# A decode kernel's tail: last weight load in six transfers, output rows in four column groups gathered in PSUM, one copy and two stores at the end

## The chip, the cores and the metric

The kernel runs on one core of one Trainium2 chip. The metric is the device time of one execution in microseconds; lower is better. The span of a profile is about 2 us shorter than the time of the same run, because the time also holds what lies outside the profiled span. In the profile's lines PE is TensorE, PEld its weight loads, DVE VectorE, ACT ScalarE, POOL GpSimd and SP SyncE; a q behind a name is that engine's instruction queue, which issues transfers. SBUF is the on-chip memory of 128 partitions, PSUM the one that PE writes its products to. The granted clock is the share of PE's full clock that the chip allowed in a stretch.

## The reference, cut to what matters

```python
x = A_x                                             # (2, 1, 1024), batch of two, one token
g = sigmoid((x * gate_w).sum(-1, keepdims=True))
a = attention(x, k_cache, v_cache, wq) @ wo         # 32 heads, 16384 cached keys of 128, for each of two batches
b = mixer_mlp(B: x, w1..w4)                         # ends as x1 + h2
return g * a + (1 - g) * b                          # (2, 1, 1024)
```

The two caches are 537 MB together in bf16; with the weights the kernel reads 570 MB, each byte once. The last thing that happens is `o @ wo`: a (2 x 4096) by (4096 x 1024) product whose 8 MB of weights are the last bytes to be loaded.

## The kernel before

All large loads go through a ring of four 4 MB slots in SBUF, issued from one queue (SyncE) in a fixed order: weights of the projections, then keys and values of 64 (head, batch) pairs, last `wo` in two loads of 4 MB. The second of these is cut in three transfers of 3, 0.5 and 0.5 MB, each with a semaphore of its own, so that the products can start before all is there:

```python
wloads[("wo", pi)] = [wo_load(k0, kn - 1), wo_load(k0 + kn - 1, 1, 0, 2), wo_load(k0 + kn - 1, 1, 2, 2)]
wo_chunks.append(((("wo", pi), 0), [(c, r) for c in range(k0, k0 + kn - 1) for r in range(R4)]))
for t in range(2):
    wo_chunks.append(((("wo", pi), 1 + t), [(k0 + kn - 1, 2 * t + r) for r in range(2)]))
```

The output rows of the two batches are cut in halves of 512 columns. Half `hf` stands on PSUM partitions `32*hf` and `32*hf+1`, so the two matmuls of a weight row use two column groups of the PE array. (`c, r` name a row block of 128 weight rows: 4 `c` times 4 `r` in one load of 4 MB.)

```python
for c, r in crs:
    for hf in range(2):
        ev = pl.add("pe", lambda e, ...: e.matmul(
            rows_ps[32 * hf:32 * hf + 2, 0:HD2], lhsT=OT4_sb[:, r, c, :], rhs=wt[:, c % CPS, r, hf * HD2:(hf + 1) * HD2],
            start=first, stop=True, tile_position=(0, 32 * hf), ...), waits=w, sig=True)
```

The gate and the other half of the sum come in with the last VectorE instruction; then two stores, one from SyncE's queue and one from ScalarE's, each of two partitions:

```python
for hf, eng in enumerate(("sp", "act")):
    sl = slice(32 * hf, 32 * hf + 2)
    if hf == 0:
        ev_fin = pl.add("dve", lambda e: e.scalar_tensor_tensor(orow[:, :], rows_ps[0:PR, 0:HD2], grow[0:PR, 0:1], bgrow[:, :],
                                                                op0=ALU.mult, op1=ALU.add), waits=(ev_alast, evd["bg"]), sig=True)
    ev_out = pl.dma(eng, lambda e, sl=sl, hf=hf: e.dma_start(out[:, 0, hf * HD2:(hf + 1) * HD2], orow[sl, :]), s_out[hf],
                    waits=(ev_fin,))
```

## Time and profile before

| what | value |
|---|---|
| time, median of the first three runs | 1333.75 us (1333.74 to 1333.94) |
| profiled span | 1332.0 us |
| DMA engines busy | 99.7% of 16 engines' span |
| last byte of the last load | 1328.23 us |
| from there to the start of the last VectorE instruction | 1.24 us |
| that instruction | 0.74 us |
| from its end to the end of the span | 1.75 us |

From the page of the kernel before: the busy tenths and GB/s of the DMA engines in 40 slices of the span, the packets of the load queue and of the instruction queue (count, MB, share), and one group of VectorE instructions (count, busy time, mean ns).

```profile
span 1332.0 us, 13845 instructions
...
DMA  9999999999999999999999999999999999999998
GB/s 403 428 428 432 431 432 434 428 434 429 434 432 432 433 429 433 430 434 432 432 433 428 433 431 433 433 429 435 428 434 431 431 435 429 432 430 435 431 429 337
...
q1 hardware_dynamic: 21428, 570.44, 99.7%
q8 instruction: 10, 0.16, 0.0%
...
L726 DVE TENSOR_SCALAR OTp<-ps,recip 128x1 bf16<-128x1 f32 x64 | 14.1, 221 | 162.8 <-PE ps L710 162.8
...
```

The DMA engines are full from the second slice to the second last, and the bytes are fixed. So what the other engines compute in the middle should not show in the time (the length of their programs can: e7 and e8 below). The last slice moves 337 GB/s, so the tail is where something can be had. The end of the chain of waits of the kernel before (start us, duration us, what):

```profile
...
1300.87 24.87 DMA ring<-in_A_wo_dram
...
1325.79 3.66 PE ps L747 x32
...
1329.47 0.74 DVE orow L780
```

And the same stretch in the timeline (start us, duration us, engine, line, operation, tiles, count; in brackets the idle time before it and what ended it):

```profile
...
1325.79 3.62 PE L747 MATMUL ps<-ring,OT_sb 128*2 128x512 bf16 x32 [2.56 <-DMA ring<-in_A_wo_dram]
1329.47 0.74 DVE L780 SCALAR_TENSOR_TENSOR orow<-ps,grow,bgrow 34x512 bf16<-34x512 f32 x1 [15.25 <-PE ps L747]
1330.24 0.33 SPq L782 DMA_DIRECT2D out_dram<-orow  x1
1330.25 0.26 ACTq L782 DMA_DIRECT2D out_dram<-orow  x1
```

PE starts when the 3 MB part is complete and works 3.66 us through the 32 matmuls of the load. The chain names only this first part. The trace's records of each DMA engine's completion tell the rest: the 0.5 MB parts are complete at 1326.99 and 1328.23, while PE still works on the first part. So PE ends at 1329.45, 1.22 us after the last byte.

### The profile page before, as it was taken

Reading aid. Unit: us, or ns where it says so; the run is one execution under the profiler, and the core shown is the slowest. Engines: PE = TensorE matmul, PEld = TensorE weight load, DVE = VectorE, ACT = ScalarE, POOL = GpSimd, SP = SyncE. Lnnn points to the kernel's source line nnn. Section 1 sums busy time; section 2 is a strip of 40 time slices with the busy share of each in tenths; the row PEclk is TensorE's granted clock in tenths of the full one; section 3 lists DMA queues with packets and bytes.
Section 4 is the critical chain, followed back from the end, with each engine's and each line's share of the span. In section 5 each row is a group of like instructions: output and inputs, shape, how many; then the busy total and the mean of one; then the engine's idle time right before and its main releaser. Section 6 shows DMA issues by size and latency. Waiting matters only on the chain.

```text
span 1332.0 us, 13845 instructions
## 1 busy us (share of the span) xinstructions
PE 853.7 (64%) x5330; PEld 332.3 (25%) x5330; DVE 758.9 (57%) x998; ACT 89.7 (7%) x195; POOL 33.0 (2%) x161
## 2 busy tenths in 40 slices
PE   3656666667666666766666666666666666666765
PEld 3322222222222222222222222222222222222222
DVE  1076566556656656665665566566556656655661
ACT  0000000000000000000000000000000000000000
POOL 2000000000000000000000000000000000000000
PEclk9989887788787879787887887887899697878877
DMA  9999999999999999999999999999999999999998
GB/s 403 428 428 432 431 432 434 428 434 429 434 432 432 433 429 433 430 434 432 432 433 428 433 431 433 433 429 435 428 434 431 431 435 429 432 430 435 431 429 337
DMA packets 21459, 570.64 MB, mean 428 GB/s; under 512 B 2235, under 2 KB 2243, under 8 KB 2502
## 3 DMA queue, kind: packets, MB, share of 16 engines
q1 hardware_dynamic: 21428, 570.44, 99.7%
q8 instruction: 10, 0.16, 0.0%
q14 instruction: 3, 0.02, 0.0%
q10 hardware_dynamic: 18, 0.01, 0.0%
HBM read 570.44 MB, written 0.00 MB: 428 GB/s over the span
## 4 chain that ended last, share of the span: by engine, by line
DMA 65%; PE 22%; DVE 11%; issue 2%; DVEq 0%; ACT 0%; POOL 0%; SPq 0%
DMA ring<-in_A_k_cache_dram 62%; PE ps L643 20%; DVE ring L631 10%; DMA ring<-in_A_wo_dram 2%; DMA ring<-in_A_wq_dram 2%; DVE OTp L726 1%; PE ps L460 0%; PE ps L747 0%; PE ps L589 0%; PE ps L489 0%; PE ps L710 0%; PE ps L381 0%; DVEq L71 0%; ACT P_sb L696 0%; DVE orow L780 0%
## 5 line engine op out<-in xcount | busy, mean ns | idle before, releaser
L643 PE MATMUL ps<-ring,Z 128*128 128x512 bf16 x2048 | 642.0, 467 | 338.9 <-DVE ring L631 328.3
L631 DVE STREAM_TRANSPOSE ring<-ring 128x1024 f32<-128x1024 f32 x512 | 590.9, 1211 | 129.2 <-DMA ring<-in_A_k_cache_dram 129.2
L643 PEld LDWEIGHTS ps<-ring,Z 128*128 128x128 bf16 x2048 | 206.8, 112 | 701.6 <-issue 358.8
L659 PE MATMUL ps<-ring,PT_sb 128*32 128x512 bf16 x2048 | 123.9, 384 | 3.1 <-DMA ring<-in_A_v_cache_dram 3.1
L696 ACT ACTIVATE P_sb<-ps,negm 128x512 bf16<-128x512 f32 x64 | 44.0, 687 | 1118.0 <-DVE negm L690 1118.0
L726 DVE TENSOR_SCALAR OTp<-ps,recip 128x1 bf16<-128x1 f32 x64 | 14.1, 221 | 162.8 <-PE ps L710 162.8
L668 DVE TENSOR_REDUCE rA<-ps 128x1 f32<-128x512 f32 x64 | 44.2, 691 | 90.0 <-PE ps L643 90.0
L702 DVE STREAM_TRANSPOSE PT_sb<-P_sb 128x512 bf16<-128x512 bf16 x64 | 45.5, 711 | 54.1 <-ACT P_sb L696 54.1
L659 PEld LDWEIGHTS ps<-ring,PT_sb 128*32 128x32 bf16 x2048 | 49.1, 97 | 46.8 <-issue 4.6
L675 PE MATMUL ps<-ident,rmax_bf 128*1 128x128 bf16 x64 | 13.9, 217 | 66.3 <-DVE rmax_bf L670 66.3
L705 ACT ACTIVATE acc_sb<-ps 128x512 bf16<-128x512 f32 x64 | 38.2, 597 | 55.1 <-PE ps L659 55.1
L728 POOL COPY OT_sb<-OTp 128x1 bf16<-128x1 bf16 x64 | 11.9, 186 | 1204.7 <-DVE OTp L726 1204.7
L675 PEld LDWEIGHTS ps<-ident,rmax_bf 128*1 128x1 bf16 x64 | 5.1, 79 | 97.9 <-DVE rmax_bf L670 97.9
L680 DVE TENSOR_REDUCE m_sb<-ps 1x1 bf16<-1x128 bf16 x64 | 18.0, 281 | 19.8 <-PE ps L675 19.8
L710 PEld LDWEIGHTS ps<-dsel,acc_sb 128*128 128x128 bf16 x256 | 20.4, 118 | 33.9 <-issue 30.0
L690 DVE TENSOR_SCALAR negm<-ps,cAB 128x1 f32<-128x1 f32 x64 | 17.7, 277 | 17.3 <-PE ps L685 17.3
L685 PE MATMUL ps<-m_sb,ones_bf 1*128 1x1 bf16 x64 | 11.0, 172 | 24.1 <-DVE m_sb L680 24.1
L717 PEld LDWEIGHTS ps<-rowsum,ones_f 128*128 128x128 f32 x128 | 19.0, 188 | 28.0 <-issue 26.8
L717 PE MATMUL ps<-rowsum,ones_f 128*128 128x1 f32 x128 | 24.5, 260 | 1.2 <-ACT P_sb L696 1.2
L722 DVE RECIPROCAL recip<-ps 128x1 f32<-128x1 f32 x64 | 10.7, 167 | 20.0 <-PE ps L717 20.0
L589 PE MATMUL ps<-xT_bf,ring 128*128 128x2 bf16 x256 | 7.1, 165 | 17.9 <-DMA ring<-in_A_wq_dram 17.9
L710 PE MATMUL ps<-dsel,acc_sb 128*128 128x1 bf16 x256 | 17.5, 172 | 1.1 <-ACT acc_sb L705 1.1
(91 smaller groups left out, 128.5 us busy)
## 6 DMA issues: line engine op xcount, KB each, us to landing
ring<-in_A_k_cache_dram SPq DMA_DIRECT2D x64, 4096.0 KB, 25.7
ring<-in_A_v_cache_dram SPq DMA_DIRECT2D x64, 4096.0 KB, 31.7
ring<-in_A_wq_dram SPq DMA_DIRECT2D x2, 4096.0 KB, 17.6
ring<-in_B_w_dram SPq DMA_DIRECT2D x2, 3584.0 KB, 32.4
ring<-in_B_w_dram SPq DMA_DIRECT2D x1, 4096.0 KB, 28.3
ring<-in_A_wo_dram SPq DMA_DIRECT2D x1, 4096.0 KB, 33.7
ring<-in_B_w_dram SPq DMA_DIRECT2D x1, 3072.0 KB, 27.4
ring<-in_A_wo_dram SPq DMA_DIRECT2D x1, 3072.0 KB, 24.9
```

What stands on the lines that cost most here:

```text
L631: ev_T[(g, u)] = pl.add("dve", lambda e: e.transpose(ap, ap), waits=(arrived(("k", g)),), sig=True)
L643: ev = pl.add("pe", lambda e, bp=bp: e.matmul(S_ps(pg)[:, 0:NCOL], lhsT=Z[:, pg, bp, ZO - 2 * u:ZO - 2 * u + P], rhs=kv[:, :, bp // 2, :, ...
L659: ev = pl.add("pe", lambda e, jj=jj, hf=hf, cg=cg: e.matmul(acc_ps[32 * cg:32 * cg + 32, 0:512], lhsT=PT_sb[:, pg, 32 * jj:32 * jj + 32], ...
L668: e1 = pl.add("dve", lambda e: e.tensor_reduce(rA[:, pg:pg + 1], S_ps(pg)[:, 0:NCOL], axis=AX.X, op=ALU.max), waits=(ev_S[g],), sig=True)
L675: ev_mt[g] = pl.add("pe", lambda e: e.transpose(mt_ps, rmax_bf[:, pg:pg + 1], ident[:, :]), waits=(ev_rmax[g], ev_m.get(g - 1), ev_ident i ...
L680: ev_m[g] = pl.add("dve", lambda e: e.tensor_reduce(m_sb[0:1, pg:pg + 1], mt_ps, axis=AX.X, op=ALU.max), waits=(ev_mt[g], ev_mb.get(g - 2) ...
L696: ev_P[g] = pl.add("act", lambda e: e.activation(P_sb[:, pg, :], S_ps(pg)[:, 0:NCOL], ACT.Exp, bias=negm[:, pg:pg + 1], scale=scale, accum ...
L702: ev_PT[g] = pl.add("dve", lambda e: e.transpose(PT_sb[:, pg, :], P_sb[:, pg, :]), waits=(ev_P[g], ev_PV.get(g - 2)), sig=True)
L705: ev_accc[g] = pl.add("act", lambda e: e.activation(acc_sb[:, :], acc_ps[:, 0:512], ACT.Copy), waits=(ev_PV[g], ev_ext.get(g - 1)), sig=True)
L710: ev = pl.add("pe", lambda e, w=w: e.matmul(oT_ps, lhsT=acc_sb[:, w * P:(w + 1) * P], rhs=dsel[:, w:w + 1], start=(w == 0), stop=(w == 3)) ...
L717: ev_l[g] = pl.add("pe", lambda e: e.matmul(l_ps, lhsT=ones_f[:, :], rhs=rowsum[:, pg:pg + 1], start=True, stop=True), waits=(ev_P[g], ev_ ...
L726: ev_OT[g] = pl.add("dve", lambda e: e.tensor_scalar(OTp[:, pg:pg + 1], oT_ps, recip[:, pg:pg + 1], None, op0=ALU.mult), waits=(ev_ext[g], ...
```

## The change

The intent: let PE follow the arriving bytes more closely (six transfers, the last one a quarter of a megabyte), do the row products in four column groups of 256 in place of two of 512, and make the last VectorE instruction shorter. For the last, the gate is folded into the normalisation of the heads, the other half of the sum, already gated, is written into the PSUM bank before the output products add to it, and only a copy of 256 columns remains. The diff, cut to its core:

```diff
-                wloads[("wo", pi)] = [wo_load(k0, kn - 1), wo_load(k0 + kn - 1, 1, 0, 2), wo_load(k0 + kn - 1, 1, 2, 2)]
-                ...
+                parts = [(c, 0, R4) for c in range(k0, k0 + kn - 1)] + [(k0 + kn - 1, 0, 2)]
+                parts += [(k0 + kn - 1, r, 1) for r in range(2, R4)]
+                wloads[("wo", pi)] = [wo_load(c, 1, r0, rn) for c, r0, rn in parts]
 ...
-            evd["bg"] = ... e.tensor_scalar(bgrow[:, :], bgrow[:, :], grow[0:PR, 1:2], None, op0=ALU.mult)
+            evd["bg"] = ... e.tensor_scalar(rows_ps[:, 0:DQ], bgrow[:, :], grow[:, 0:1], None, op0=ALU.mult)
 ...
-            ... e.tensor_scalar(OTp[:, pg:pg + 1], oT_ps, recip[:, pg:pg + 1], None, op0=ALU.mult)
+            ... e.tensor_scalar(OTp[:, pg:pg + 1], oT_ps, recip[:, pg:pg + 1], gT[:, pg:pg + 1], op0=ALU.mult, op1=ALU.mult)
 ...
-                    for hf in range(2):
-                            rows_ps[32 * hf:32 * hf + 2, 0:HD2], ..., rhs=wt[:, c % CPS, r, hf * HD2:(hf + 1) * HD2], start=first, ...
+                    for qd in range(NQ):                                # NQ = 4, DQ = 256
+                            rows_ps[32 * qd:32 * qd + 2, 0:DQ], ..., rhs=wt[:, c % CPS, r, qd * DQ:(qd + 1) * DQ], start=False, ...
 ...
-                ev_fin = ... e.scalar_tensor_tensor(orow[:, :], rows_ps[0:PR, 0:HD2], grow[0:PR, 0:1], bgrow[:, :], ...)
-            ev_out = ... e.dma_start(out[:, 0, hf * HD2:(hf + 1) * HD2], orow[sl, :])
+        ev_fin = pl.add("dve", lambda e: e.tensor_copy(orow[0:PR, :], rows_ps[0:PR, 0:DQ]), waits=(ev_alast,), sig=True)
+            ev_out = ... e.dma_start(out[b, 0, :].rearrange("(q n) -> q n", q=NQ), orow[b:PR:32, :])
```

The row products of the prologue (second mixer) go to four groups of 256 as well, and the input row comes in four small loads in place of two.

More of the change, by code (lines that the diff above doesn't have):

```diff
@@ L150, in build_kernel @@
     CPS = SLOT // (R4 * D)
-    HD2 = D // 2
-    PR = 34
-    assert H % HPC == 0 and HD2 <= 512
+    NQ = 4
+    DQ = D // NQ
+    PR = 32 * (NQ - 1) + 2
+    assert H % HPC == 0 and DQ <= 512
     with ExitStack() as st:
@@ L188, in build_kernel @@
         OT4_sb = sb("OT4_sb", [P, R4, NCT, 2], BF16)
-        xrow = sb("xrow", [PR, HD2], BF16)
-        bgrow = sb("bgrow", [PR, HD2], F32)
-        orow = sb("orow", [PR, HD2], BF16)
-        m22 = sb("m22", [P, 2, 2], F32)
+        xrow = sb("xrow", [P, DQ], BF16)
+        bgrow = sb("bgrow", [P, DQ], F32)
+        orow = sb("orow", [P, DQ], BF16)
+        m24 = sb("m24", [P, 2, NQ], F32)
         m2 = sb("m2", [P, 2], F32)
-        gm = sb("gm", [P, 2, 2], F32)
-        grow = sb("grow", [P, 2], F32)
+        gm = sb("gm", [P, 2], F32)
+        grow = sb("grow", [P, 1], F32)
         zz = sb("zz", [P, 2, NBD, 2], F32)
@@ L217, in build_kernel @@
         s_xr = sem("dxr")
-        s_tail = [sem(f"dtl{i}") for i in range(3)]
+        s_tail = [sem(f"dtl{i}") for i in range(CPS + 2)]
         pl = _Plan(esems)
@@ L251, in build_kernel @@
         pconst(lambda e: e.memset(Z[:, :, :, :], 0.0))
-        e0 = pconst(lambda e: e.memset(m22[:, :, :], 0.0))
-        pconst(aff(m22[:, :, :], 0, [[-1, 2], [-32, 2]], 1), (e0,))
+        e0 = pconst(lambda e: e.memset(m24[:, :, :], 0.0))
+        pconst(aff(m24[:, :, :], 0, [[-1, 2], [-32, NQ]], 1), (e0,))
         ev_xr0 = pconst(lambda e: e.memset(xrow[:, :], 0.0))
@@ L257, in build_kernel @@
                     waits=(ev_rowm,), sig=True)
-        pl.add("dve", lambda e: e.tensor_reduce(m2[:, :], m22[:, :, :], axis=AX.X, op=ALU.add), waits=(ev_const,))
+        pl.add("dve", lambda e: e.tensor_reduce(m2[:, :], m24[:, :, :], axis=AX.X, op=ALU.add), waits=(ev_const,))
         pl.add("dve", lambda e: e.tensor_scalar(cAB[:, 0:1], rowv[:, :], -scale, None, op0=ALU.mult), waits=(e0,))
@@ L329, in build_kernel @@
             else:
-                wloads[("wo", pi)] = [wo_load(k0, kn - 1), wo_load(k0 + kn - 1, 1, 0, 2), wo_load(k0 + kn - 1, 1, 2, 2)]
-                wo_chunks.append(((("wo", pi), 0), [(c, r) for c in range(k0, k0 + kn - 1) for r in range(R4)]))
-                for t in range(2):
-                    wo_chunks.append(((("wo", pi), 1 + t), [(k0 + kn - 1, 2 * t + r) for r in range(2)]))
+                parts = [(c, 0, R4) for c in range(k0, k0 + kn - 1)] + [(k0 + kn - 1, 0, 2)]
+                parts += [(k0 + kn - 1, r, 1) for r in range(2, R4)]
+                wloads[("wo", pi)] = [wo_load(c, 1, r0, rn) for c, r0, rn in parts]
+                for t, (c, r0, rn) in enumerate(parts):
+                    wo_chunks.append(((("wo", pi), t), [(c, r0 + r) for r in range(rn)]))
         def q_load(key):
@@ L395, in st_gate @@
                               waits=(e4,), sig=True)
-            e5 = pl.add("dve", lambda e: e.tensor_tensor(gm[:, :, :], gT[:, :].rearrange("p (t b) -> p t b", b=2),
-                                                         m2[:, :].unsqueeze(1).broadcast_to([P, 2, 2]), op=ALU.mult),
+            e5 = pl.add("dve", lambda e: e.tensor_tensor(gm[:, :], gT[:, 2:4], m2[:, :], op=ALU.mult),
                         waits=(evd["g"], ev_const), sig=True)
-            evd["grow"] = pl.add("dve", lambda e: e.tensor_reduce(grow[:, :], gm[:, :, :], axis=AX.X, op=ALU.add), waits=(e5,), sig=True)
+            evd["grow"] = pl.add("dve", lambda e: e.tensor_reduce(grow[:, :], gm[:, :], axis=AX.X, op=ALU.add), waits=(e5,), sig=True)
         def ln_a(z_ap, zkey, st_ps, tag):
@@ L487, in run @@
                 for kl in kls:
-                    for hf in range(2):
-                        ev = pl.add("pe", lambda e, kl=kl, hf=hf, st=row_first[0]: e.matmul(
-                            rows_ps[32 * hf:32 * hf + 2, 0:HD2], lhsT=lhs_of(k0 + kl), rhs=wv[:, kl, hf * HD2:(hf + 1) * HD2],
-                            start=st, stop=True, tile_position=(0, 32 * hf), skip_group_check=True),
-                            waits=w, sig=(kl == kls[-1] and hf == 1))
+                    for qd in range(NQ):
+                        ev = pl.add("pe", lambda e, kl=kl, qd=qd, st=row_first[0]: e.matmul(
+                            rows_ps[32 * qd:32 * qd + 2, 0:DQ], lhsT=lhs_of(k0 + kl), rhs=wv[:, kl, qd * DQ:(qd + 1) * DQ],
+                            start=st, stop=True, tile_position=(0, 32 * qd), skip_group_check=True),
+                            waits=w, sig=(kl == kls[-1] and qd == NQ - 1))
                         w = ()
@@ L501, in st_bg @@
             evs = []
-            for hf in range(2):
-                sl = slice(32 * hf, 32 * hf + 2)
-                c1 = pl.add("dve", lambda e, sl=sl: e.tensor_tensor(bgrow[sl, :], rows_ps[sl, 0:HD2], xrow[sl, :], op=ALU.add),
-                            waits=(evd["rows"], ev_xr, ev_bg0), sig=True)
-                evs.append(c1)
-            evd["bg"] = pl.add("dve", lambda e: e.tensor_scalar(bgrow[:, :], bgrow[:, :], grow[0:PR, 1:2], None, op0=ALU.mult),
+            for qd in range(NQ):
+                sl = slice(32 * qd, 32 * qd + 2)
+                evs.append(pl.add("dve", lambda e, sl=sl: e.tensor_tensor(bgrow[sl, :], rows_ps[sl, 0:DQ], xrow[sl, :], op=ALU.add),
+                                  waits=(evd["rows"], ev_xr, ev_bg0), sig=True))
+            evd["bg"] = pl.add("dve", lambda e: e.tensor_scalar(rows_ps[:, 0:DQ], bgrow[:, :], grow[:, 0:1], None, op0=ALU.mult),
                                waits=tuple(evs) + (evd["grow"],), sig=True)
@@ L543, in build_kernel @@
         ev_gw = pl.dma("act", lambda e: e.dma_start(gw_row[0:1, :], gate_w.rearrange("(o d) -> o d", o=1)), s_gw)
-        for hf in range(2):
-            ev_xr = pl.dma("act", lambda e, hf=hf: e.dma_start(xrow[32 * hf:32 * hf + 2, :], A_x[:, 0, hf * HD2:(hf + 1) * HD2]), s_xr,
+        for qd in range(NQ):
+            ev_xr = pl.dma("act", lambda e, qd=qd: e.dma_start(xrow[32 * qd:32 * qd + 2, :], A_x[:, 0, qd * DQ:(qd + 1) * DQ]), s_xr,
                            waits=(ev_xr0,))
@@ L725, in do_OT @@
             pg = g % 2
-            ev_OT[g] = pl.add("dve", lambda e: e.tensor_scalar(OTp[:, pg:pg + 1], oT_ps, recip[:, pg:pg + 1], None, op0=ALU.mult),
+            ev_OT[g] = pl.add("dve", lambda e: e.tensor_scalar(OTp[:, pg:pg + 1], oT_ps, recip[:, pg:pg + 1], gT[:, pg:pg + 1], op0=ALU.mult,
+                                                               op1=ALU.mult),
                               waits=(ev_ext[g], ev_rc[g], ev_OTc.get(g - 2)), sig=True)
@@ L740, in do_aproj @@
             ev_o4 = pl.add("dve", lambda e: e.tensor_copy(OT4_sb[:, :, :, :], o4_ps), waits=(ev,), sig=True)
-            first = True
             for (key, k), crs in wo_chunks:
@@ L745, in do_aproj @@
                 for c, r in crs:
-                    for hf in range(2):
-                        ev = pl.add("pe", lambda e, c=c, r=r, hf=hf, wt=wt, first=first: e.matmul(
-                            rows_ps[32 * hf:32 * hf + 2, 0:HD2], lhsT=OT4_sb[:, r, c, :], rhs=wt[:, c % CPS, r, hf * HD2:(hf + 1) * HD2],
-                            start=first, stop=True, tile_position=(0, 32 * hf), skip_group_check=True), waits=w, sig=True)
+                    for qd in range(NQ):
+                        ev = pl.add("pe", lambda e, c=c, r=r, qd=qd, wt=wt: e.matmul(
+                            rows_ps[32 * qd:32 * qd + 2, 0:DQ], lhsT=OT4_sb[:, r, c, :], rhs=wt[:, c % CPS, r, qd * DQ:(qd + 1) * DQ],
+                            start=False, stop=True, tile_position=(0, 32 * qd), skip_group_check=True), waits=w,
+                            sig=(qd == NQ - 1))
                         w = ()
-                    first = False
             return ev
@@ L776, in build_kernel @@
         ev_alast = do_aproj()
-        for hf, eng in enumerate(("sp", "act")):
-            sl = slice(32 * hf, 32 * hf + 2)
-            if hf == 0:
-                ev_fin = pl.add("dve", lambda e: e.scalar_tensor_tensor(orow[:, :], rows_ps[0:PR, 0:HD2], grow[0:PR, 0:1], bgrow[:, :],
-                                                                        op0=ALU.mult, op1=ALU.add), waits=(ev_alast, evd["bg"]), sig=True)
-            ev_out = pl.dma(eng, lambda e, sl=sl, hf=hf: e.dma_start(out[:, 0, hf * HD2:(hf + 1) * HD2], orow[sl, :]), s_out[hf],
+        ev_fin = pl.add("dve", lambda e: e.tensor_copy(orow[0:PR, :], rows_ps[0:PR, 0:DQ]), waits=(ev_alast,), sig=True)
+        for b, eng in enumerate(("sp", "act")):
+            ev_out = pl.dma(eng, lambda e, b=b: e.dma_start(out[b, 0, :].rearrange("(q n) -> q n", q=NQ), orow[b:PR:32, :]), s_out[b],
                             waits=(ev_fin,))
```

## The prediction

> **What bounds the kernel now.** The DMA engines. The page gives queue 1 99.7% of 16 engines' span; the 40 slices move 428 to 435 GB/s, only the first (403) and last (337) less. PE is 64% busy, VectorE 57%. Loads land 25 to 32 us after issue while one 4 MB load moves in under 10, so more than one is always queued. The 570 MB do not change. Only the tail after the last bytes is to be had.
>
> **The tail before** (chain of waits, timeline, the trace's records of each DMA engine's completion). The 3 MB part of the last load is complete at 1325.74, the two 512 KB parts at 1326.99 and 1328.23. PE starts its 32 matmuls of that load at 1325.79 and ends at 1329.45 (0.114 us each), because 24 of them wait for the 3 MB: 1.22 us after the last byte. The fused multiply-add takes 0.74 us, to 1330.21; stores and their completion 1.75 us, to 1331.96. Sum after the last byte: 3.73 us.
>
> **What the change does.**
> - Transfers of 1, 1, 1, 0.5, 0.25, 0.25 MB: PE works through each while the next lands; after the last one only 4 matmuls (256 columns, four column groups) remain. The Trainium skill (TensorEngine Tiling, Tiling Modes) lists four independent 128x32 tiles; this trace agrees: the PV product with four groups takes 1.94 us for 32 matmuls of 512 columns, the output rows with two groups 3.66. Estimate for 4 of 256: 0.3 us (one of 512 is shown as 0.38). PE ends 0.35 us after the last byte in place of 1.22. Gain 0.87.
> - One copy of 98x256 from PSUM in place of the 34x512 multiply-add (743 ns). A cast of 64 columns from PSUM took 225 ns, a reduction over 512 took 691: 1.04 ns a column, so 425 ns. Gain 0.31.
> - Stores: two as before, four rows of 512 B in place of two of 1 KB: still 1.75 us.
> - Last byte: 8 KB packets take 314 ns, 4 KB 159; 2 KB about 82, so two quarter transfers cost 0.04 us more than one half.
> - Twice as many row matmuls, the extra scalar in the 221 ns normalisation, two more small input loads: off the path, behind queued DMA.
>
> **A risk in the last byte.** One engine completes 1.4 us after the fifteenth: a 16 KB instruction packet (1.07 us) went through it at 1288; another at 1316 set a second engine back. The Trainium skill (Runtime: NRT & Kernel Launch, Instruction fetch mechanics) says that instructions come in 16 KiB blocks; the trace has ten such packets. PE gets 272 more instructions, about one block. If it lands late on an engine already behind, the last byte comes up to 1.2 us later and eats the gain. More likely it falls on another engine and costs nothing.
>
> **Sum.** 3.73 becomes 0.35+0.02+0.43+1.75+0.04 = 2.6 us: 1.1 us less, 1332.6 us. Range 1331.5 to 1333.9. Faster by over 2%: 0.0; within 2%: 0.99; slower: 0.01.
>
> **What would show it.** Timeline: last row matmuls end 0.3 to 0.5 us after the last wait for output weights (now 3.66); the copy 0.40 to 0.45 us; from there to the end 1.7 to 1.8; last byte at 1328.2 to 1328.4. DMA share and 430 GB/s unchanged in the middle slices.
>
> **What would make it wrong.** The extra instruction block on a lagging engine; narrow matmuls limited by issue, so that PE is behind when the last part lands; slower 2 KB packets; slower stores from four partitions; a chip with another DMA rate.

## The result

| | before | after |
|---|---|---|
| time, median | 1333.83 us (1333.74 to 1333.94, 4 runs) | 1333.45 us (1333.23 to 1333.55, 4 runs) |
| profiled span | 1332.0 us | 1331.4 us |

The ratio is 0.9997 with a 95% interval of 0.998 to 1.0014. A ratio here is the mean time of one kernel's fast runs over that of the other's in the same rounds, so it is not quite the ratio of the medians. In a later session (five runs, e0 below) the change came out at 1333.37 against 1334.12 us. It gains 0.4 to 0.7 us where 1.1 was predicted; both gains are smaller than the half width of the ratio's interval (0.0013 or more, which is 1.7 us), so the terms of the profile have to carry the argument.

The page after, the same lines:

```profile
span 1331.4 us, 14124 instructions
...
DMA  9999999999999999999999999999999999999998
GB/s 401 431 425 433 433 428 435 428 434 432 432 431 428 437 429 432 432 431 434 428 432 432 432 432 429 433 432 432 431 430 435 430 431 433 432 431 430 433 431 344
...
q1 hardware_dynamic: 21608, 570.44, 99.7%
q8 instruction: 11, 0.18, 0.1%
...
L727 DVE TENSOR_SCALAR OTp<-ps,recip,gT 128x1 bf16<-128x1 f32 x64 | 17.9, 280 | 159.9 <-PE ps L711 159.9
...
```

The middle slices are as before, and PE's instructions now come in 11 blocks of 16 KB in place of 10. The normalisation of the heads went from 221 to 280 ns, 3.8 us more of VectorE in all, and none of it shows. The end of the chain and of the timeline:

```profile
...
1305.21 22.96 DMA ring<-in_A_wo_dram
...
1328.21 0.41 PE ps L748 x4
...
1328.65 0.42 DVE orow L778
```

```profile
...
1318.25 3.90 PE L748 MATMUL ps<-ring,OT_sb 128*2 128x256 bf16 x80 [4.72 <-DMA ring<-in_A_wo_dram]
...
1325.71 1.02 PE L748 MATMUL ps<-ring,OT_sb 128*2 128x256 bf16 x16 [1.88 <-DMA ring<-in_A_wo_dram]
...
1328.21 0.38 PE L748 MATMUL ps<-ring,OT_sb 128*2 128x256 bf16 x4 [0.25 <-DMA ring<-in_A_wo_dram]
1328.65 0.42 DVE L778 CAST orow<-ps 98x256 bf16<-98x256 f32 x1 [14.84 <-PE ps L748]
1329.10 0.65 SPq L780 DMA_DIRECT2D out_dram<-orow  x1
1329.10 0.59 ACTq L780 DMA_DIRECT2D out_dram<-orow  x1
```

The last byte lands at 1328.17 as against 1328.23. PE has 4 matmuls left and ends 0.45 us later, no longer 1.22. The copy takes 0.42, no longer 0.74. Up to here the change has won 1.15 us (the copy ends at 1329.07, the multiply-add ended at 1330.22). But the span ends 2.35 us after the copy, where it ended 1.75 us after the multiply-add. In the timeline the two stores take 0.65 and 0.59 us to issue, no longer 0.33 and 0.26. The two stores give back 0.6 of 1.15 us.

### The profile page after: what moved, and what is told of

Same layout as the page of the kernel before. It is cut to its first block, busy times and chain, and to the rows that moved or that the text cites. A ratio compares the mean times of both kernels' runs of the same rounds, so it can differ in the third digit from the quotient of the medians.

```text
span 1331.4 us, 14124 instructions
## 1 busy us (share of the span) xinstructions
PE 860.8 (65%) x5466; PEld 343.8 (26%) x5466; DVE 762.6 (57%) x1000; ACT 89.7 (7%) x195; POOL 32.9 (2%) x161
## 4 chain that ended last, share of the span: by engine, by line
DMA 64%; PE 25%; DVE 8%; issue 2%; SPq 0%; DVEq 0%; ACT 0%; POOL 0%
DMA ring<-in_A_k_cache_dram 61%; PE ps L644 23%; DVE ring L632 7%; DMA ring<-in_A_wo_dram 2%; DMA ring<-in_A_wq_dram 2%; DVE OTp L727 1%; PE ps L461 0%; PE ps L590 0%; SPq L312 0%; PE ps L711 0%; PE ps L490 0%; PE ps L383 0%; DVEq L71 0%; ACT P_sb L697 0%; POOL mv L424 0%
## 5 line engine op out<-in xcount | busy, mean ns | idle before, releaser
L644 PE MATMUL ps<-ring,Z 128*128 128x512 bf16 x2048 | 655.6, 480 | 326.0 <-DVE ring L632 320.2
L644 PEld LDWEIGHTS ps<-ring,Z 128*128 128x128 bf16 x2048 | 216.6, 114 | 692.5 <-issue 376.3
L727 DVE TENSOR_SCALAR OTp<-ps,recip,gT 128x1 bf16<-128x1 f32 x64 | 17.9, 280 | 159.9 <-PE ps L711 159.9
```

Of the source, the lines that this page charges most:

```text
L644: ev = pl.add("pe", lambda e, bp=bp: e.matmul(S_ps(pg)[:, 0:NCOL], lhsT=Z[:, pg, bp, ZO - 2 * u:ZO - 2 * u + P], rhs=kv[:, :, bp // 2, :, ...
L727: ev_OT[g] = pl.add("dve", lambda e: e.tensor_scalar(OTp[:, pg:pg + 1], oT_ps, recip[:, pg:pg + 1], gT[:, pg:pg + 1], op0=ALU.mult, op1=AL ...
```

## The experiments

**Theories.** A: the stores lost it. A1: because each now reads partitions 32 apart. A2: because each now has four rows of 512 B. B: more and smaller transfers at the end cost something of their own. C: something else ate it: a late last byte, through the extra instruction block (a risk that the prediction named). D, E and F came up on the way: D over the last byte (e7, e8), E and F over the four column groups (e10, e11).

All numbers of the table are from each run's profile, in us; "time" is the mean of the kernel's runs less the mean of the kernel before in the same session (its means there: 1334.08, 1333.91, 1334.02, 1334.12; each of these four sessions ran on another chip).

| run | time | last byte | last byte to VectorE start | VectorE | VectorE end to span end |
|---|---|---|---|---|---|
| before | | 1328.23 | 1.24 | 0.74 | 1.75 |
| after | -0.41 | 1328.17 | 0.48 | 0.42 | 2.35 |
| e0_after_again | -0.69 | 1328.45 | 0.48 | 0.42 | 2.28 |
| e1_split_only | -0.77 | 1328.28 | 0.50 | 0.74 | 1.76 |
| e2_store_pairs | -0.95 | 1328.52 | 0.48 | 0.43 | 2.07 |
| e3_two_groups_copy | -0.88 | 1328.31 | 0.49 | 0.68 | 1.76 |
| e4_before_strided_stores | +0.58 | 1328.21 | 1.25 | 0.74 | 2.34 |
| e9_four_adjacent | -1.09 | 1328.10 | 0.48 | 0.42 | 1.85 |
| e5_no_split | +0.06 | 1328.22 | 1.18 | 0.42 | 2.29 |
| e6_two_copies | -1.19 | 1328.51 | 0.49 | 0.42 | 1.77 |
| e7_more_blocks | +1.58 | 1329.84 | 1.25 | 0.74 | 1.74 |
| e8_fewer_blocks | -1.41 | 1326.85 | 1.25 | 0.74 | 1.75 |
| e10_half_columns | -0.68 | 1328.45 | 0.48 | 0.42 | 2.38 |
| e11_keep_busy | -0.72 | 1328.28 | 0.48 | 0.42 | 2.37 |

All ratios to the kernel before lie between 0.9989 and 1.0012, and their intervals are 0.0013 to 0.0017 wide to either side: they resolve none of these steps. What resolves them are the profiles, whose terms repeat to within 0.1 us, except for the last byte, which wanders by 0.4 us between kernels with ten or eleven instruction blocks (1328.10 to 1328.52). The times of one kernel lie within 0.2 to 0.8 us of each other. The differences of the means put the kernels in nearly the same order as the profiles' spans, but are up to 0.5 us larger than a single pair of spans gives; 0.2 of that lies outside the span (see Open), and the rest is no more than runs of one kernel differ by.

### e0_after_again: the change once more

No edit. 

> The changed kernel once more, as the yardstick beside the next three. Theory A (the four-row, 32-apart stores cost 0.6 us more than the old two-row ones) and theory C (the gain was lost to a late last byte through the extra instruction block) differ here: A expects the last load to land within 0.1 us of the kernel before's 1328.2 again and from the end of the copy to the end of the span 2.3 to 2.4 us (before: 1.75 from the end of the multiply-add). C expects the last landing to move by a microsecond between runs. Time: 0.3 to 0.5 us under the kernel before.

Measured: 1333.37 us (1333.08 to 1333.92) against 1334.12. The last byte came 0.28 us later than in the first profile, not a microsecond as C expects (A expected it within 0.1 us); the store term was 2.28. The gain of 0.7 is above the 0.3 to 0.5 expected. Theory A holds so far.

### e1_split_only: only the six transfers

```diff
 # the kernel before, and:
+                parts = [(c, 0, R4) for c in range(k0, k0 + kn - 1)] + [(k0 + kn - 1, 0, 2)]
+                parts += [(k0 + kn - 1, r, 1) for r in range(2, R4)]
+                wloads[("wo", pi)] = [wo_load(c, 1, r0, rn) for c, r0, rn in parts]
```

> The kernel before with only the six-way split of the last load; two column groups, multiply-add and two-row stores kept. Theory A: last byte at 1328.2, then two matmuls of 512 columns (about 0.45 us with the wait), multiply-add 0.74, stores 1.75: end 2.96 us after the last byte where the kernel before has 3.73. So 0.75 us under the kernel before and about 0.3 under the whole change. Rival C (last byte) or B (a plain cost of more, smaller transfers at the end): the split brings a later last byte and the gain is 0.4 us or less.

The end of its timeline:

```profile
...
1328.33 0.38 PE L748 MATMUL ps<-ring,OT_sb 128*2 128x512 bf16 x2 [0.25 <-DMA ring<-in_A_wo_dram]
1328.78 0.74 DVE L781 SCALAR_TENSOR_TENSOR orow<-ps,grow,bgrow 34x512 bf16<-34x512 f32 x1 [14.57 <-PE ps L748]
1329.55 0.33 SPq L783 DMA_DIRECT2D out_dram<-orow  x1
...
```

Every term as expected: 2 matmuls of 512 columns take as long as 4 of 256 did (0.38 us, but at a granted clock of 1.00 here and of 0.50 in the change), the old multiply-add 0.74, the old stores 1.76. One part of the change, with the rest left as it was, gains as much as the whole (span mean 1331.34 against 1331.56). The smaller transfers cost nothing that shows: the last byte comes at 1328.28 here and at 1328.10 to 1328.52 in all kernels of ten or eleven blocks with the split, at 1328.21 to 1328.45 in those without. The Trainium skill (DMA: Bandwidth & Descriptors, Bandwidth) advises batching DMAs to at least 1 MiB, from a table measured on transfers that GpSimd issued; behind a queue that is never empty, the quarter-megabyte transfers that SyncE issued here, in rows of 2 KB, cost less than this scatter shows.

### e2_store_pairs: four stores of two neighbouring rows

```diff
 # the kernel after, and:
-            ev_out = ... e.dma_start(out[b, 0, :].rearrange("(q n) -> q n", q=NQ), orow[b:PR:32, :])      # one on each queue
+            for qd in (k, k + 2):                                                                          # two on each queue
+                ev_out = ... e.dma_start(out[:, 0, qd * DQ:(qd + 1) * DQ], orow[32 * qd:32 * qd + 2, :])
```

> The changed kernel with four stores of two neighbouring rows of 512 B, two on each queue, in place of two stores of four rows 32 apart. Theory A1 (it is the stride over partitions that makes the store slow): each store issues in 0.26 to 0.33 us again, the second on a queue follows 0.35 later, copy to end 2.1 us, 0.25 us under the changed kernel. Theory A2 (it is the number of rows or of 512 B packets, stride or not): no gain, copy to end 2.35 or more.

Measured: copy to end 2.07 us, as A1 said: the single stores issue in 0.33 and 0.26 us again, and the second of each queue follows. The form of the store is the cost. But these stores have two rows each, so the number of rows is not ruled out as the cause. That needs e4 and e9.

### e3_two_groups_copy: everything of the change but the four groups

```diff
 # e1, and the gate in the heads and the other half in PSUM as in the change, with two groups of 512:
+            evd["bg"] = ... e.tensor_scalar(rows_ps[0:PR, 0:HD2], bgrow[:, :], grow[0:PR, 1:2], None, op0=ALU.mult)
+                ev_fin = ... e.tensor_copy(orow[:, :], rows_ps[0:PR, 0:HD2])
```

> Six-way split, gate folded into the heads and gated other half in PSUM as in the change, but two column groups of 512, so that one copy of 34x512 and the old two-row stores of 1 KB remain. Theory A: two matmuls 0.45, copy of 512 columns from PSUM about 0.69 (1.04 ns a column and 0.16), stores 1.75: end 2.9 us after the last byte, 0.85 us under the kernel before, 0.35 under the whole change. If narrow groups were what gains and stores cost nothing, it would be slower than the whole change by 0.3.

Measured: the copy takes 0.68 us and the stores 1.76, 2.93 us after the last byte in all. The expected gain of 0.85 came out at 0.88. Against the whole change it is 0.44 us less of span mean (1331.12 against 1331.56), but only 0.19 us less of time. Folding the gate is worth 0.06 us when the width stays: the multiply-add was nearly a copy already.

### e4_before_strided_stores and e9_four_adjacent: stride or rows

```diff
 # e4: the kernel before, with its stores cut by batch
-    e.dma_start(out[:, 0, hf * HD2:(hf + 1) * HD2], orow[sl, :])
+    e.dma_start(out[hf, 0, :].rearrange("(q n) -> q n", q=2), orow[hf:PR:32, :])
 # e9: the kernel after, wrong on purpose
-    orow[b:PR:32, :]
+    orow[0:NQ, :]
```

> The kernel before, with its two stores cut by batch instead of by half: each takes two rows of 1 KB that lie 32 partitions apart. Theory A1 (a stride over partitions makes the store slow): issue 0.6 us as in the changed kernel in place of 0.26 to 0.33, multiply-add to end 2.3 us in place of 1.75, 0.55 us over the kernel before. Theory A2 (four rows in one store make it slow): issue 0.26 to 0.33, multiply-add to end 1.75, the time of the kernel before.

> The changed kernel, wrong on purpose: its two stores each read the first four neighbouring rows in place of four rows 32 apart; same rows and bytes in each store. A1 (stride): issue back to about 0.3, copy to end 1.75 us, 0.6 us under the changed kernel. A2 (four rows in one store): issue 0.6, copy to end 2.3 us, the changed kernel's time.

The ends of the timelines of e4, then of e9:

```profile
...
1329.46 0.74 DVE L780 SCALAR_TENSOR_TENSOR orow<-ps,grow,bgrow 34x512 bf16<-34x512 f32 x1 [15.48 <-PE ps L747]
1330.23 0.63 SPq L782 DMA_DIRECT2D out_dram<-orow  x1
1330.23 0.59 ACTq L782 DMA_DIRECT2D out_dram<-orow  x1
```

```profile
...
1328.58 0.42 DVE L778 CAST orow<-ps 98x256 bf16<-98x256 f32 x1 [14.61 <-PE ps L748]
1329.03 0.35 SPq L780 DMA_DIRECT2D out_dram<-orow  x1
1329.04 0.28 ACTq L780 DMA_DIRECT2D out_dram<-orow  x1
```

In e4 the rows are two, of 1 KB, as before, but 32 partitions apart. (Each store also writes a whole row of one batch in place of half a row of both, so the destination differs too. In e9 the destination is the change's and the stores are fast, so it is not the destination.) Issue goes from 0.33 and 0.26 to 0.63 and 0.59 us, and the tail from 1.75 to 2.34. In e9 the rows are four, of 512 B, as in the change, but neighbours. Issue goes back to 0.35 and 0.28, the tail to 1.85 (0.1 more than expected: four rows may cost that much). So A1: it is the partition stride of the source, 32 being the only one tried. It costs 0.59 us with two rows (e4) and 0.43 to 0.53 with four (the five kernels with the change's stores, 2.28 to 2.38, against e9). (e9 gives a wrong result, as it must.)

The packets tell where the time sits. From the start of the issue to the first packet of the earlier store pass 0.75 us in the kernel before and 1.24 in the change. The Trainium skill (DMA: Bandwidth & Descriptors, Latency and other measured facts) gives about 600 ns to the first byte on this path; the first of these agrees roughly, the second is twice that. The page has nothing on a partition stride. What the queue does with a stride in that time no run here shows.

### e5_no_split: the whole change but the split, and a surprise

```diff
 # the kernel after, with the three transfers of before
+                wloads[("wo", pi)] = [wo_load(k0, kn - 1), wo_load(k0 + kn - 1, 1, 0, 2), wo_load(k0 + kn - 1, 1, 2, 2)]
```

> The whole change without its split: parts of 3, 0.5 and 0.5 MB again, with four column groups and one copy. Four groups do 16 matmuls of 256 columns in 0.6 us where the kernel before did 8 of 512 in 0.9, so the 48 of the first part end about 1.9 us after it lands at 1325.7, before the last part lands at 1328.2; then 8 matmuls, about 0.5 us. Expected: PE ends 0.5 to 0.6 us after the last byte, so the split adds only 0.1 us to four groups, and the time is within 0.15 us of the changed kernel. If narrow matmuls are limited by issue, PE ends over 1 us after the last byte and the time is 0.5 us over the changed kernel.

My expectation failed: 1333.97 us, no gain over the kernel before. The products of the last two loads in its timeline:

```profile
...
1318.37 3.58 PE L747 MATMUL ps<-ring,OT_sb 128*2 128x256 bf16 x64 [4.45 <-DMA ring<-in_A_wo_dram]
...
1325.81 3.54 PE L747 MATMUL ps<-ring,OT_sb 128*2 128x256 bf16 x64 [3.86 <-DMA ring<-in_A_wo_dram]
...
```

64 matmuls of 256 columns in four groups took 3.54 us, 0.055 each, as long as 32 of 512 in two groups. Either there is a floor of 0.055 us for a pair of weight load and matmul (F), or the clock is to blame (E). The stretches of the kernel before and of e5 (us, length, then busy time and count of PE, weight load, VectorE, ScalarE, GpSimd; granted clock, DMA share, GB/s):

```profile
...
1322.00:1324.00 2.00, 1.23 (x12) 0.33 (x8) 0.00 (x0) 0.00 (x0) 0.00 (x0) 1.00 0.98 399
1324.00:1325.75 1.75, 0.00 (x0) 0.00 (x0) 0.00 (x0) 0.00 (x0) 0.00 (x0) 1.00 0.73 295
1325.75:1327.75 2.00, 1.96 (x20) 0.81 (x22) 0.00 (x0) 0.00 (x0) 0.00 (x0) 1.00 0.18 74
...
```

```profile
...
1322.00:1324.00 2.00, 0.00 (x0) 0.00 (x0) 0.00 (x0) 0.00 (x0) 0.00 (x0) 0.92 1.01 403
1324.00:1325.75 1.75, 0.00 (x0) 0.00 (x0) 0.00 (x0) 0.00 (x0) 0.00 (x0) 1.00 0.71 290
1325.75:1327.75 2.00, 1.94 (x40) 1.26 (x44) 0.00 (x0) 0.00 (x0) 0.00 (x0) 0.50 0.22 90
...
```

In the kernel before, PE is still at work on the first load until 1323.2, and idles 2.56 us before the last one; the clock is 1.00 when it starts. In e5 the first load's products end at 1321.95, PE idles 3.86 us, and the clock is at 0.50 right after it starts again. The Trainium skill (TensorE: Matmul & The Clock Gate, What's actually happening) says that an idle window of about 3.4 us brings the array to half clock and that as much sustained work brings it back. The idle times of these two kernels fit. Two runs test it.

### e10_half_columns and e11_keep_busy: floor or clock

```diff
 # e10: e5, wrong on purpose: half of each matmul's columns
-    rows_ps[32 * qd:32 * qd + 2, 0:DQ], ..., rhs=wt[:, c % CPS, r, qd * DQ:(qd + 1) * DQ]
+    rows_ps[32 * qd:32 * qd + 2, 0:DQ // 2], ..., rhs=wt[:, c % CPS, r, qd * DQ:qd * DQ + DQ // 2]
 # e11: e5, with 12 dead matmuls between the products of the first and of the second load
+    if ci == 1:
+        for _ in range(12):
+            pe_b5(lambda e: e.matmul(banks[5][:, 0:512], lhsT=ident[:, :], rhs=PermQ[...], start=True, stop=True, ...), ...)
```

> Why did four column groups gain PE nothing without the split (64 matmuls of 256 columns took 3.54 us, the same as 32 of 512 in two groups before)? This is that version, wrong on purpose: each of the 128 output matmuls streams 128 columns in place of 256, same number of matmuls and weight loads. Theory E (the granted clock, 0.50 in that stretch where the kernel before had 1.00, halves the streaming): the last 64 take about 1.8 to 2.0 us. Rival F (a floor of 0.055 us for each pair of weight load and matmul): 3.5 us again, time unchanged against the version without the split.

> The version without the split, with 12 dead matmuls of 512 columns (a constant, into a PSUM bank that is free by then) between the first and the last load's products, so that PE does not idle for 3.9 us there. Theory E (PE idles longer because four groups finish the first load sooner, and the idle stretch brings the clock down to half): the granted clock is 1.00 when the last load's matmuls start at 1325.8, the first 48 take under 1.5 us, PE ends 0.5 us after the last byte in place of 1.13, and the time falls by 0.6 us against the version without the split. Rival F (floor of 0.055 us a pair): clock 1.00 perhaps, but 64 matmuls still in 3.5 us, no gain.

The last load's products in e10, timeline and stretch:

```profile
...
1326.00 1.66 PE L747 MATMUL ps<-ring,OT_sb 128*2 128x128 bf16 x56 [5.54 <-DMA ring<-in_A_wo_dram]
...
1325.75:1327.75 2.00, 1.66 (x56) 1.28 (x56) 0.00 (x0) 0.00 (x0) 0.00 (x0) 0.50 0.29 117
...
```

e10 ran 56 matmuls in 1.66 us and then waited for the last part, at a granted clock of 0.50: 0.03 us each. There is no floor of 0.055 us; F falls. e11, stretches and timeline:

```profile
...
1322.00:1324.00 2.00, 2.00 (x6) 0.71 (x7) 0.00 (x0) 0.00 (x0) 0.00 (x0) 0.60 1.01 403
1324.00:1325.75 1.75, 1.50 (x7) 0.49 (x5) 0.00 (x0) 0.00 (x0) 0.00 (x0) 1.00 0.72 295
1325.75:1327.75 2.00, 1.70 (x56) 1.21 (x56) 0.00 (x0) 0.00 (x0) 0.00 (x0) 1.00 0.28 115
...
```

```profile
...
1321.91 0.13 PEld L747 LDWEIGHTS ps<-PermQ,ident 128*128 128x128 bf16 x2 [0.43 <-PE ps L751]
...
1325.84 1.70 PE L751 MATMUL ps<-ring,OT_sb 128*2 128x256 bf16 x56 [0.34 <-DMA ring<-in_A_wo_dram]
...
1328.32 0.39 PE L751 MATMUL ps<-ring,OT_sb 128*2 128x256 bf16 x8 [0.78 <-DMA ring<-in_A_wo_dram]
...
```

With the 12 dead matmuls the clock is 1.00, 56 matmuls take 1.70 us, PE waits for the last part and ends 0.46 us after the last byte. The time falls to 1333.37 us, 0.72 under the kernel before where e5 was 0.06 over it. E holds: **by finishing the first load sooner, four column groups made the idle stretch that took half of the clock away, and that cancelled what they gained.** At an equal clock they do halve PE's time: at 1.00 the 64 products of a load would take about 1.9 us (an estimate from 56 in 1.70), where two groups took 3.62. With the split little of this counts, because only 4 matmuls are left after the last byte. The clock was lost in the change, too: its trace has 0.50 from 1324.87 to the end, after a stretch of 3.41 us (1321.46 to 1324.87) in which PE never idled longer than 1.1 us at a time but was busy for only 1.30. So a wholly idle window was not needed.

One thing about e10: it leaves out half of the output product and still passed the comparison with the reference. The comparison is therefore blind to errors of that size in the gated attention term, in this and in the other runs.

### e7_more_blocks and e8_fewer_blocks: what sets the last byte

The prediction's risk was that an extra 16 KB instruction block might set a lagging DMA engine back further. It had not (1328.17 after, 1328.23 before). What places the last byte at all?

```diff
 # e7: the kernel before, loop over heads entered at 20, so the programs of PE, VectorE and ScalarE are longer
-        GL, GE = 4, G - 2
+        GL, GE = 20, G - 2
 # e8: the kernel before, wrong on purpose: one block of output columns in the mixer's dense products, all loads kept
-                for nb in range(nout):
+                for nb in range(1):
```

> What sets the last byte? The kernel before with its loop over heads entered at 20 in place of 4: the same work, but PE's program is about 16 x 142 instructions longer, which is 8 to 9 instruction blocks of 16 KB more (10 before, 18 or 19 here). Theory D (the blocks pass in turn through eight of the sixteen DMA engines, each pass sets its engine back 1.2 us for good, so the last byte lands as late as the engine hit most often): three hits on some engine in place of two, last byte at 1329.3 to 1329.6 in place of 1328.2, time 1.1 to 1.4 us over the kernel before. Rival (blocks spread over all sixteen engines, or a delayed engine catches up): last byte and time unchanged within 0.3 us.

> The kernel before, wrong on purpose: of the two dense products of the second mixer only the first block of 128 output columns is computed, all loads kept. PE's program is 544 instructions shorter, so eight blocks in place of ten. Theory D: no DMA engine is hit twice, the engines' last completions lie within 2.1 us of each other in place of 3.3, the last byte lands at 1327.0 in place of 1328.2, and the time falls by 1.1 to 1.3 us with not a byte less loaded. Rival: last byte unchanged within 0.3 us.

The instruction queue's packets in e7, then in e8 (count, MB, share):

```profile
...
q8 instruction: 19, 0.31, 0.1%
...
```

```profile
...
q8 instruction: 8, 0.13, 0.0%
...
```

For the last transfer, the trace's completions of the 16 DMA engines, as delay behind the first of them:

| kernel | blocks of 16 KB | up to 1.05 us | 1.2 to 2.2 | 2.8 to 3.4 | 4.5 to 5.0 | last byte |
|---|---|---|---|---|---|---|
| e8_fewer_blocks | 8 | 7 | 9 | 0 | 0 | 1326.85 |
| before | 10 | 7 | 7 | 2 | 0 | 1328.23 |
| after | 11 | 7 | 6 | 3 | 0 | 1328.17 |
| e7_more_blocks | 19 | 7 | 0 | 6 | 3 | 1329.84 |

Two blocks above eight put two engines one step further back, three blocks put three, and three above sixteen put three engines two steps further back. That is what a turn through eight of the engines gives. (A ninth engine lags in all of them, and by one step more in e7. The 8 KB instruction packets would fit, three within the span of the other kernels of this table and six in that of e7, but no run tests that.) The trace does not name the engine of a packet or of a completion; that it is one and the same engine which stays behind is read from delays that keep their size from load to load. So read, an engine once set back does not catch up: in the changed kernel the engine hit a second time at 181 us is 3.1 us behind the first at the load that lands at 191 us and 3.2 behind at the one that lands at 1308 us. The last byte waits for the engine that was hit most often. So the extra block of the change was free because it was the eleventh and, by this pattern, went to an engine with one hit. Without hits nine and ten the same bytes are in 1.4 us sooner: e8 is 1.41 us faster than the kernel before, e7 1.58 slower. Both are a little over what I expected (1.1 to 1.3, and 1.1 to 1.4): a hit costs 1.4 to 1.6 us, not 1.2.

The Trainium skill (Runtime: NRT & Kernel Launch, Instruction fetch mechanics) says that PE's instructions come in 16 KiB blocks and that the cost of crossing one is mostly hidden. The trace agrees on the size. On the cost it does not where the DMA engines are the limit: whether PE itself ever waited for a block no run here tests; the DMA engine that carried one was set back and the last byte came later.

### e6_two_copies: a better tail

```diff
 # e3, with the quarters of a row in two PSUM banks, copied by VectorE and ScalarE at the same time, stores of two neighbouring rows
+    ev_fin = ... "dve", e.tensor_copy(orow[:, 0:HC], rowsb[0][0:PR, 0:HC])
+    ev_fi2 = ... "act", e.activation(orow[:, HC:HD2], rowsb[1][0:PR, 0:HC], ACT.Copy)
```

> A try for the best tail: split in six, two column groups, each row's two quarters in two PSUM banks, so that VectorE copies 34x256 from one while ScalarE copies 34x256 from the other, and the old stores of two neighbouring rows of 1 KB. Expected: four matmuls of 256 columns in 0.45 us, copies 0.43 (ScalarE about 0.4), stores 1.75: 2.65 us after the last byte, 0.25 us under the version with one copy of 512 columns, 1.05 under the kernel before. If ScalarE's copy takes 0.6 as its 512-column one does, the gain over that version is under 0.1.

The form with two banks (one dead matmul pair sets the second bank up) ran at 1332.71 us (1332.37 to 1333.04), 1.19 us under the kernel before. VectorE takes 0.42 and ScalarE 0.38 us, stores 1.77, so 2.68 us after the last byte, as expected (2.65):

```profile
...
1329.00 0.38 ACT L792 ACTIVATE orow<-ps 34x256 bf16<-34x256 f32 x1 [16.00 <-PE ps L757]
1329.00 0.42 DVE L791 CAST orow<-ps 34x256 bf16<-34x256 f32 x1 [14.47 <-PE ps L757]
...
```

It is the fastest kernel here that passed the comparison and does the whole work: its slowest run (1333.04) is below the fastest of the kernel before in the same session (1333.61). Against the change, which ran in other sessions, it gains 0.5 to 0.8 us more over the kernel before.

**Open.** The difference between time and span is 2.0 us for the kernel before and 1.8 for the change, e2, e5, e6, e9, e10 and e11; e1, e3, e4, e7 and e8 are at 2.0 to 2.1. So 0.2 us of the gain of the change lies outside the profiled span. I did not find out where. The eight kernels at 1.8 are those with eleven instruction blocks; those with eight, ten and nineteen are at 2.0 to 2.1. No run tests whether the blocks are the reason.

## Why the prediction was right or wrong

"Within 2%" and the range (1331.5 to 1333.9) were right, but the range also holds the time of the kernel before (1333.83), so it would have been right without any gain. The gain was 0.4 to 0.7 us in place of 1.1. Point by point:

- *"Only the tail after the last bytes is to be had"*: right. 3.8 us more work on VectorE and twice as many row matmuls in the prologue left all slices but the first, the third (425) and the last at 428 to 437 GB/s.
- *"PE ends 0.35 us after the last byte in place of 1.22"*: right in kind, 0.1 small. It was 0.45: four matmuls of 256 columns took 0.41 us with the hand-over, not 0.3.
- *"One copy of 98x256 ... 425 ns"*: right, 424.
- *"Stores: two as before, four rows of 512 B in place of two of 1 KB: still 1.75 us"*: **this step failed.** It measured 2.35 (2.28 in the repeat). I compared bytes and rows. Slower stores from four partitions were on the list of what would make it wrong, but got no size, and the distance of the partitions was not considered: 32 in the change, neighbours before. e4 and e9 show that the stride alone makes 0.4 to 0.6 us of it; the rest, about 0.1, may be the four rows.
- *"Last byte: ... two quarter transfers cost 0.04 us more"* and the risk of the extra block: right that neither would show. That the block would more likely fall on another engine was a guess, and it was lucky as far as the prediction goes; the pattern of e7 and e8 explains it afterwards.
- *"the PV product with four groups takes 1.94 us for 32 matmuls"* as evidence that four groups run twice as fast: true at an equal clock. In the tail of the change, as in e5, the clock was 0.50 where the kernel before had 1.00, and that takes the factor back (e5, e11). It did little harm to the sum, as the split leaves so few matmuls.

With the store term at its measured size the sum is 0.48 + 0.42 + 2.35 = 3.25 us after the last byte, in place of 2.6 predicted and 3.73 before. The profile's gain of 0.54 us is the difference of the first and the last, and 0.06 of an earlier last byte.

## What to carry to other kernels

At the end of a kernel count what follows the last byte, term by term, and for a store count its partitions' distance as well as its bytes: here a layout that made the copy 0.3 us shorter made the stores 0.6 us longer. Test the parts of a change alone; here the split by itself gained as much as the whole. Where DMA is the limit, look at the length of the programs too: here the blocks of PE's instructions rode on the same DMA engines, and nine more of them came with 1.6 us.

## What the Trainium skill lacked or had wrong

- DMA: Bandwidth & Descriptors lacks the cost of a source with a stride over partitions. For a stride of 32: issue 0.59 to 0.65 us in place of 0.26 to 0.35, first packet 1.24 us after the start of the issue in place of 0.75, and to the end 0.59 us more with two rows (e4), 0.43 to 0.53 with four (against e9).
- DMA: Bandwidth & Descriptors, Bandwidth: the advice to batch to 1 MiB does not say what holds behind a full queue; transfers of 256 KB at its end cost nothing that shows (last byte 1328.10 to 1328.52 with them, 1328.21 to 1328.45 without).
- Runtime: NRT & Kernel Launch, Instruction fetch mechanics: "mostly hidden" does not hold for a kernel limited by DMA. Eight, ten and nineteen blocks of 16 KB gave a last byte at 1326.85, 1328.23 and 1329.84 us, and a pattern over the engines that fits a turn through eight of them.
- TensorE: Matmul & The Clock Gate agreed with what was seen in e5 and e11 (0.50 after 3.86 us of idle time, 1.00 when kept busy). In the change 0.50 also followed a window of 3.41 us with PE busy for 1.30. The page has no warning that work done faster can lengthen the idle stretch and so lose the clock: 64 matmuls in 3.54 us, and 56 of the same in 1.70 with 12 dead ones put before them.
